# A fused Fourier filter, feed-forward block and expert layer: three steps of the token loop put in another order, and a single-buffered DMA turn in the last pair

## The chip, the core and the metric

The kernel runs on one core of one Trainium2 chip. The metric is the device time of one execution in microseconds. TensorE is called PE here, VectorE DVE, ScalarE ACT, GpSimd POOL and SyncE SP.

## What is computed

```python
def reference(x, filt_r, filt_i, w_in, w_out, g_ln, expert_emb, tau, w1, w2):
    X = np.fft.rfft(x, axis=1)                      # x is 8 x 3072 x 256
    x = np.fft.irfft(X * (filt_r + 1j * filt_i), n=3072, axis=1).reshape(24576, 256)
    h = x @ w_in                                    # 256 -> 1024
    e = np.exp(h - h.max(-1))
    solu = h * e / e.sum(-1)
    ln = (solu - solu.mean(-1)) / np.sqrt(solu.var(-1) + 1e-6) * g_ln
    x = ln @ w_out                                  # 1024 -> 256
    logits = unit(x) @ unit(expert_emb).T / tau     # 8 experts
    k = argmax(logits);  gate = softmax(logits)[k]
    return gate * (relu(x @ w1[k]) @ w2[k])         # 256 -> 1024 -> 256
```

The products are made to nearly float32 accuracy from float16 halves: a value is split into a high half and the remainder, and three products of halves take the place of one.

## The kernel before

The eight sequences are worked on as four pairs. A pair goes through a transform in four stages (64 x 48 points): `fft` holds stages 1 to 3 with the filter between the second and the third, `inv4` is stage 4. Then come 48 tiles of 128 tokens in the token loop `stage_b`, and when all 192 tiles are through, `stage_c` runs the experts, block by block of 256 tokens of one expert.

The token loop (L959) runs over `i`, with two tiles in hand: tile `i`, and tile `j = i - 3`, which is three behind. For a tile:

- `begin` is the first layer: 12 matmuls into `h`, a PSUM tile of which there are two. `top` takes its maximum (DVE, `nm`, L925 and L926) and from it a scale (POOL, `gcc`, L928 and L929).
- the exponential into `es` (ACT, L967), and the product of it with `h` (DVE, also `es`, L968); the sum of its squares (ACT, `jk`, L995).
- `es` has to be turned and split into halves `T` for the second layer. `turn` (L931) does it on PE: 8 transposes back into `h` (L936), the high half on ACT (L939), the low half on DVE (L940). `send` (L942) makes the halves `hl` first, on ACT (L946) and DVE (L947), and `post` (L950) turns both by one DMA transpose from SP (L955). Before, even tiles are turned on PE and odd ones sent by DMA, but all 48 tiles of the last pair are turned on PE.
- the second layer: 24 matmuls into `o` (L983), whose last 8 columns are the logits. Then the square of the row (ACT, L1001), its inverse root as a scale `c2` (POOL, `gcc`, L1009), the logits' copy `graw` (DVE, L1007), and one tile later, in `half`, the row split and stored (`rows`, L1013 and L1014; `put`, L1018).

Stage 4 makes two tiles of tokens at a time, on even `i`: 8 matmuls into a PSUM tile `a` (L740), of which there are two that the transform's stages use as well, then the high half `xh` on ACT (L745) and the low one, `xh` too in the rows, on DVE (L746).

Eight tiles make a group. `b_final` picks their experts and places: a generator that goes a step further with each `i`, some of it on POOL (a reciprocal root in 16 small operations, L808 to L811) and with a small matmul that counts (L851, L853; it reads `goh`). A group marked `slow` takes its POOL work in smaller pieces. Each token's place is scattered into a list in DRAM (L166). One group is marked `snap`: the counts behind it fix the first 24 blocks of the experts, whose table `first_slots` (the generator `early`) reads from the list (L1098, tile `crow`) and whose first block it gathers (L1169) and turns (L1174, tile `cxT`), a step with each `i` from `i >= n - N2 + SPLIT + LAG`, which is 185, on.

Between these, `aux` does other work in two pieces per tile, one ahead of the first layer and one behind it. In the first three pairs that is the next pair's stages 1 to 3 and the maxima of the expert weights (L423); in the last pair it is the split of the expert weights into halves (`w_split`: loads L440 and L442, ACT L462, DVE L454), until tile 38 of the pair. Its loads are two steps ahead.

Nothing reorders this: each engine runs its instructions in the order in which the code issues them, and waits where an input isn't there. What is written ahead of what in the loop is the order on every engine and queue, SP's and POOL's too. Tiles come from pools by tag with a fixed number of buffers. The last pair has its own pool `bp`, in the room that the transforms leave.

```python
            if 0 <= i - 1 < n and i != n - 1:
                (turn if i % 2 or i > n - N2 else send)(i - 1)
```

Of the kernel before, what the change touches and what calls it, by code (L numbers as in the profile page):

```python
# [12 lines left out]
I32 = mybir.dt.int32  # L13
# [140 lines left out]
class Build:  # L154
# [734 lines left out]
    def stage_b(self, xp, bps, gp, ps, hp, op, aux, early):  # L889
# [8 lines left out]
        def over(f, x):  # L898

            while x in (2, 3):  # L900
                x = next(f)
            return x
# [56 lines left out]
        for i in range(n + LAG):  # L959
            j = i - LAG  # L960
            now = 0 <= i < n
            if 0 <= i - 1 < n and i != n - 1:
                (turn if i % 2 or i > n - N2 else send)(i - 1)
            if now:
                L = live[i]
                L["s"] = L["pool"].tile([128, FF], F32, name="es", tag="es")
                nc.scalar.activation(L["s"], L["h"], AF.Exp, bias=L["nm"], scale=self.isc_h[:, i // N2:i // N2 + 1], accum_out=col(i, "st", 0))  # L967
                nc.vector.scalar_tensor_tensor(L["s"], L["h"], col(i, "cc", 0), L["s"], op0=ALU.mult, op1=ALU.mult, accum_out=col(i, "st", 1))  # L968
            if i == n - 1:
                turn(i - 1)  # L970
            if i % 2 == 0:
                xs.append(next(src, None))
            if half:
                half()
                half = None
            self.catch_up()
            if 0 <= j < n:
                T = live.pop(j)["T"]
                o = op.tile([128, 512], F32, name="o", tag="o")
                q = 0  # L980
                for f in range(8):
                    for l, r in ((f, self.wo_h), (f, self.wo_l), (8 + f, self.wo_h)):
                        nc.tensor.matmul(o[:, :D + E], T[:, l, :], r[:, f, :], start=q == 0, stop=q == 23)  # L983
                        q += 1
                self.spot = o[:, 272:344]
                finals = [(f, next(f) if x == 2 else x) for f, x in finals]
            if now:
                if 0 < i <= n - N2 and i % 2 == 0:
                    post(i - 1)
                aux(*divmod(i, N2), 0)  # L990
                if i + 1 < n:
                    begin(i + 1)
                    top(i + 1)
                jk = L["pool"].tile([128, FF], BF16, name="jk", tag="jk")
                nc.scalar.activation(jk, L["s"], AF.Square, accum_out=col(i, "st", 2))  # L995
            if 0 <= j < n:
                n2, c2 = col(j, "n2", 0), col(j, "cc", 1)
                g, k = groups[j // G], j % G
                if k % 2 == 0:
                    rows = gp.tile([128, 2, RD], I32, name="rows", tag="rows", bufs=2)  # L1000
                nc.scalar.activation(rows[:, k % 2, :].bitcast(BF16)[:, :D], o[:, :D], AF.Square, accum_out=n2)  # L1001
# [4 lines left out]
            if 0 <= j < n:  # L1006
                nc.vector.tensor_copy(g["raw"][:, k, :], o[:, D:D + E])  # L1007
                finals = [(f, next(f) if x == 3 else x) for f, x in finals]
                nc.gpsimd.tensor_scalar(c2.bitcast(I32), n2.bitcast(I32), -0.5, float(MAGIC + (8 << 23)), op0=ALU.mult, op1=ALU.add)  # L1009
# [13 lines left out]
                if k == G - 1:  # L1023
                    p, nn = divmod(j - (G - 1), N2)
                    finals.append((self.b_final(groups.pop(j // G), p, nn, gp, ps, j // G == n // G - 4, j // G < n // G - 4), 0))
            if i >= n - N2 + SPLIT + LAG:
# [3 lines left out]
        finals = [(f, over(f, x)) for f, x in finals]  # L1030
# [21 lines left out]
    def table(self, sp, tp, ps, nb, start, K, blk, out):  # L1052
# [48 lines left out]
        assert len(self.scattered["lst"]) >= (self.np_run * N2 // G - (3 if start is None else 0)) * G  # L1101
# [182 lines left out]
    def run(self):  # L1284
        tc, nc = self.tc, self.nc
        last = self.np_run - 1
        with (
# [17 lines left out]
            with (  # L1305
# [3 lines left out]
                with tc.tile_pool(name="pp", bufs=1) as pp:  # L1309
# [7 lines left out]
                    self.m1 += [ap.tile([128, 4, 128], F32, name="mt", tag="mt", bufs=3) for _ in range(2)]  # L1317
# [15 lines left out]
                def last_pool():  # L1333
# [3 lines left out]
                    bps[1] = mid.enter_context(Tags(tc, "bp", {"nm": 2, "es": 2, "jk": 1, "T": 4}))  # L1337
# [84 lines left out]
```

## Time and profile before

| | |
|---|---|
| runs | 2745.77 us median of 3 (2744.71 to 2745.79) |
| the profiled execution | 2744.74 us, span 2742.9 us |
| granted PE clock | 0.986 of full speed |
| busy in the span | PE 2620.9, DVE 1891.5, ACT 1527.3, POOL 1328.7 us |

The span runs from the first instruction to the last; the execution's own time has 1.8 us around it. In the span, the first pair's transform takes the first 200 us, the token loop the time to about 1677 us (its first three pairs, with the transforms beside them, to about 1300, the last pair from there), and the experts the rest.

A row of a timeline gives the start in us, the duration, the engine, the line, the operation, out<-in and the count; in brackets the idle time of the engine just before it and what ended it. The line numbers are those of the kernel before, except in listings of the changed one.

### The profile page before, as it was taken

The numbers are of one execution on the slowest core, as the hardware profiler recorded it, in microseconds if no ns is written. First come the engines' busy times: TensorE is split into PE (matmuls) and PEld (weight loads), VectorE is DVE, ScalarE is ACT, GpSimd is POOL, SyncE is SP. The second block draws the span as 40 slices with busy tenths as digits, with TensorE's granted clock in tenths as the row PEclk, the third lists the DMA queues.
The fourth block names the chain that finished last, engine by engine and source line by source line (L and its number), as shares of the span: only waits on it lengthen the run. The fifth ranks groups of instructions, "written<-read, shape, count | busy, mean of one in ns | idle before, by whom it ended". The sixth has DMA issues, their size and how long they took to land.

```text
span 2742.9 us, 53684 instructions
## 1 busy us (share of the span) xinstructions
PE 2620.9 (96%) x20090; PEld 2024.3 (74%) x20090; DVE 1891.5 (69%) x2971; ACT 1527.3 (56%) x2852; POOL 1328.7 (48%) x2627
## 2 busy tenths in 40 slices
PE   5889999999999999999999998999999999999998
PEld 4447666676666776666776777888888888888897
DVE  4846899868989769888788975454545454454565
ACT  2556788767877767777688863223333333333332
POOL 2000346545566446665555556644444544454444
PEclk7999999999999999999999999999999999999999
DMA  9768888799997989885344422332323332322222
GB/s 313 202 193 244 222 199 199 195 246 209 195 194 161 234 222 198 191 169 138 94 122 122 126 51 56 74 76 73 79 74 78 76 76 77 77 77 76 78 60 57
DMA packets 444118, 384.13 MB, mean 140 GB/s; under 512 B 284779, under 2 KB 366837, under 8 KB 440784
## 3 DMA queue, kind: packets, MB, share of 16 engines
q1 hardware_dynamic: 391200, 310.34, 48.0%
q0 software_dynamic: 26896, 57.21, 6.8%
q10 hardware_dynamic: 25760, 13.14, 1.9%
q8 instruction: 159, 2.61, 0.4%
q14 instruction: 103, 0.84, 0.1%
HBM read 195.67 MB, written 103.09 MB: 109 GB/s over the span
## 4 chain that ended last, share of the span: by engine, by line
PE 39%; issue 23%; POOL 20%; DVE 12%; DMA 4%; ACT 1%; POOLq 0%; SPq 0%; ACTq 0%; DVEq 0%
PE h L758 15%; PE o L983 11%; POOL crow L1169 7%; POOL out_dram L166 6%; POOL scr L165 3%; DVE nm L925 3%; PE a L514 2%; PE a L688 2%; PE h L936 2%; PE a L740 2%; POOL gcc L928 2%; DMA bufA<-out 1%; DVE T L940 1%; DVE in L586 1%; PE a L650 1%
## 5 line engine op out<-in xcount | busy, mean ns | idle before, releaser
L983 PE MATMUL o<-wo_h,T 128*128 128x264 f16 x3072 | 549.6, 276 | 0.1
L928 POOL TENSOR_SCALAR gcc<-nm 128x1 f32<-128x1 f32 x192 | 180.3, 939 | 725.3 <-DVE nm L926 485.7
L758 PE MATMUL h<-win_h,xh 128*128 128x512 f16 x1536 | 492.4, 382 | 35.1 <-DVE T L940 33.5
L1212 PE MATMUL o<-cw,chh 128*128 128x256 f16 x3152 | 522.7, 273 | 0.8 <-issue 0.8
L1245 PEld LDWEIGHTS <-cw 128*128 128x128 f16 x5184 | 471.0, 98 | 58.1 <-issue 8.3
L983 PEld LDWEIGHTS <-T 128*128 128x128 f16 x4608 | 451.0, 98 | 64.4 <-ACT rows L1001 0.3
L758 PEld LDWEIGHTS <-xh 128*128 128x128 f16 x2304 | 222.0, 98 | 317.1 <-issue 84.8
L166 POOL DMA_INDIRECT out_dram<-cot,ids x197 | 215.2, 1092 | 452.9 <-ACT cot L1215 440.6
L1212 PE MATMUL o<-cw,chl 128*128 128x256 f16 x1576 | 429.7, 273 | 3.8 <-DVE chl L1249 3.6
L983 PE MATMUL o<-wo_l,T 128*128 128x264 f16 x1536 | 423.9, 276 | 0.0
L1249 DVE SCALAR_TENSOR_TENSOR chl<-h,chh 128x512 f16<-128x512 f32 x197 | 134.6, 683 | 389.9 <-ACT chh L1248 373.3
L925 DVE TENSOR_REDUCE nm<-h 128x1 f32<-128x1024 f32 x192 | 234.5, 1221 | 150.8 <-PE h L758 150.4
L1212 PEld LDWEIGHTS <-chh 128*128 128x128 f16 x3152 | 307.4, 98 | 36.7 <-issue 1.4
L1215 ACT ACTIVATE cot<-o,fac 128x256 f32<-128x256 f32 x197 | 93.5, 475 | 413.3 <-PE o L1212 407.6
L1201 DVE COPY cw<-wexp 128x4096 f16 x216 | 275.2, 1281 | 41.1 <-PE o L1212 20.7
L1245 PE MATMUL h<-cxT,cw 128*128 128x256 f16 (+1 forms) x2592 | 292.1, 264 | 7.2 <-DMA cxT<-crow 7.1
L758 PE MATMUL h<-win_l,xh 128*128 128x512 f16 x768 | 293.1, 382 | 0.0
L1245 PE MATMUL a<-cxT,cw 128*128 128x256 f16 (+1 forms) x2592 | 291.7, 263 | 0.4 <-issue 0.4
L968 DVE SCALAR_TENSOR_TENSOR es<-h,gcc,es 128x1024 f32<-128x1024 f32 x192 | 245.7, 1280 | 37.0 <-POOL gcc L929 31.9
L967 ACT ACTIVATE es<-h,nm,isc_h 128x1024 f32<-128x1024 f32 x192 | 230.2, 1199 | 31.3 <-DVE nm L926 19.4
L995 ACT ACTIVATE jk<-es 128x1024 bf16<-128x1024 f32 x192 | 202.1, 1052 | 64.2 <-DVE es L968 63.0
L166 POOL DMA_INDIRECT lst<-gdi,gix x192 | 218.1, 1136 | 35.3 <-issue 33.0
(261 smaller groups left out, 4368.7 us busy)
## 6 DMA issues: line engine op xcount, KB each, us to landing
wst<-in_w_dram SPq DMA_DIRECT2D x128, 256.0 KB
in<-in_x_dram SPq DMA_DIRECT2D x48, 512.0 KB
in<-bufA SPq DMA_DIRECT2D x64, 384.0 KB
c<-bufC SPq DMA_DIRECT2D x96, 256.0 KB
xs<-rows SPq DMA_DIRECT2D x96, 256.0 KB
ft<-in_filt_dram SPq DMA_DIRECT2D x24, 960.0 KB
bufA<-out SPq DMA_DIRECT2D x72, 256.0 KB
zw<-z SPq DMA_DIRECT2D x96, 192.0 KB
```

Source lines behind the costliest of these rows:

```text
L166: ins = self.nc.gpsimd.indirect_dma_start(in_offset=None, **kw).ins
L758: nc.tensor.matmul(h[:, nb, :], l[:, i, db, :], r[:, db, sl], start=k == 0, stop=k == 5)
L925: nc.vector.tensor_reduce(x[:, 0:1], L["h"], axis=AX.X, op=ALU.max, negate=True)
L928: nc.gpsimd.tensor_scalar(cc, nm, nm, 1.0, op0=ALU.mult, op1=ALU.max)
L967: nc.scalar.activation(L["s"], L["h"], AF.Exp, bias=L["nm"], scale=self.isc_h[:, i // N2:i // N2 + 1], accum_out=col(i, "st", 0))
L968: nc.vector.scalar_tensor_tensor(L["s"], L["h"], col(i, "cc", 0), L["s"], op0=ALU.mult, op1=ALU.mult, accum_out=col(i, "st", 1))
L983: nc.tensor.matmul(o[:, :D + E], T[:, l, :], r[:, f, :], start=q == 0, stop=q == 23)
L995: nc.scalar.activation(jk, L["s"], AF.Square, accum_out=col(i, "st", 2))
L1169: nc.gpsimd.indirect_dma_start(out=rows[:, h, :], out_offset=None, in_=self.xs, in_offset=bass.IndirectOffsetOnAxis(ap=tab["ids"][:, h, k: ...
L1201: nc.vector.tensor_copy(w.rearrange("p (o k) -> p o k", o=1), self.wexp[:, bass.ds(e, 1), part * 4096:(part + 1) * 4096])
L1212: nc.tensor.matmul(o[:, :D], l[f // fs][:, f % fs, h * 128:(h + 1) * 128], w2[:, r, f, :], start=q == 0, stop=q == 23)
L1245: nc.tensor.matmul(t[:, i, :], w1[:, l, db, f * 128:(f + 1) * 128], xT[:, r + db, :n], start=q == 0, stop=q == 5)
```

## The change

It has four parts. In the token loop, `turn` or `send` of tile `i` moves from the beginning of the next iteration to a place directly behind `begin` and `top` of tile `i + 1`, ahead of the second piece of `aux`. Stage 4 (`next(src)`) moves ahead of the product (L968) and, of tile `j`, the square and the scale `c2` move directly behind the second layer. In the last pair odd tiles are sent by DMA as elsewhere, but for the very last tile; its pool gets one buffer `hl`. And the marked group is one earlier, with the table started three tiles earlier (at 182); at the end of the loop and behind it, a group that has its choice ready no longer issues its counting matmul in the same step. Two buffers that hold constants of the first transform are taken from the tag `wst` where they came from `mt`, of the same size.

```diff
         def over(f, x):
-            while x in (2, 3):
-                x = next(f)
-            return x
+            return next(f) if x == 3 else x
...
         for i in range(n + LAG):
             j = i - LAG
             now = 0 <= i < n
-            if 0 <= i - 1 < n and i != n - 1:
-                (turn if i % 2 or i > n - N2 else send)(i - 1)
             if now:
                 L = live[i]
                 L["s"] = L["pool"].tile([128, FF], F32, name="es", tag="es")
                 nc.scalar.activation(L["s"], L["h"], AF.Exp, bias=L["nm"], scale=self.isc_h[:, i // N2:i // N2 + 1], accum_out=col(i, "st", 0))
-                nc.vector.scalar_tensor_tensor(L["s"], L["h"], col(i, "cc", 0), L["s"], op0=ALU.mult, op1=ALU.mult, accum_out=col(i, "st", 1))
-            if i == n - 1:
-                turn(i - 1)
             if i % 2 == 0:
                 xs.append(next(src, None))
+            if now:
+                nc.vector.scalar_tensor_tensor(L["s"], L["h"], col(i, "cc", 0), L["s"], op0=ALU.mult, op1=ALU.mult, accum_out=col(i, "st", 1))
...
                 finals = [(f, next(f) if x == 2 else x) for f, x in finals]
+                n2, c2 = col(j, "n2", 0), col(j, "cc", 1)
+                g, k = groups[j // G], j % G
+                if k % 2 == 0:
+                    rows = gp.tile([128, 2, RD], I32, name="rows", tag="rows", bufs=2)
+                nc.scalar.activation(rows[:, k % 2, :].bitcast(BF16)[:, :D], o[:, :D], AF.Square, accum_out=n2)
+                nc.gpsimd.tensor_scalar(c2.bitcast(I32), n2.bitcast(I32), -0.5, float(MAGIC + (8 << 23)), op0=ALU.mult, op1=ALU.add)
             if now:
-                if 0 < i <= n - N2 and i % 2 == 0:
+                if i and i % 2 == 0:
                     post(i - 1)
...
                 nc.scalar.activation(jk, L["s"], AF.Square, accum_out=col(i, "st", 2))
-            if 0 <= j < n:
-                n2, c2 = col(j, "n2", 0), col(j, "cc", 1)
...
+                (turn if i % 2 == 0 or i == n - 1 else send)(i)
             if now:
                 aux(*divmod(i, N2), 1)
...
-                    finals.append((self.b_final(groups.pop(j // G), p, nn, gp, ps, j // G == n // G - 4, j // G < n // G - 4), 0))
-            if i >= n - N2 + SPLIT + LAG:
+                    finals.append((self.b_final(groups.pop(j // G), p, nn, gp, ps, j // G == n // G - 5, j // G < n // G - 5), 0))
+            if i >= n - N2 + SPLIT:
                 next(early, 0)
             finals = [(f, x) for f, x in ((f, next(f, 1)) for f, _ in finals) if x != 1]
         self.spot = None
-        finals = [(f, over(f, x)) for f, x in finals]
...
-                    self.m1 += [ap.tile([128, 4, 128], F32, name="mt", tag="mt", bufs=3) for _ in range(2)]
+                    self.m1 += [ap.tile([128, 4, 128], F32, name="wst", tag="wst", bufs=3) for _ in range(2)]
...
-                    bps[1] = mid.enter_context(Tags(tc, "bp", {"nm": 2, "es": 2, "jk": 1, "T": 4}))
+                    bps[1] = mid.enter_context(Tags(tc, "bp", {"nm": 2, "es": 2, "jk": 1, "hl": 1, "T": 4}))
```

How the order moves, at three places. PE near the start of the token loop, behind a first layer, before (the rows of L514 are stage 1 of the next pair, those of L936 the turn):

```order
L758 MATMUL h<-win_h,xh 128x512
L514 MATMUL a<-in,mt 128x256 x2
L936 MATMUL h<-cst,es 128x128 x8
L514 MATMUL a<-in,mt 128x256 x2
L758 LDWEIGHTS xh
```

and in the changed kernel:

```order
L758 MATMUL h<-win_h,xh 128x512
L934 MATMUL h<-cst,es 128x128 x8
L514 MATMUL a<-in,mt 128x256 x4
L758 LDWEIGHTS xh
```

The turn stands directly behind the first layer, and the transform's piece follows it. In all, the turn has 97 such rows where it had 120, and SP 95 DMA transposes of `hl` where it had 72.

DVE in the last pair, from one maximum to the next, before (`wexp` is the split of the expert weights, `T` and `hl` the low halves of a turned and of a sent tile, `xh` stage 4's):

```order
L925 TENSOR_REDUCE nm<-h 128x1
L926 TENSOR_SCALAR nm<-nm,isc_h 128x1
L454 SCALAR_TENSOR_TENSOR wexp<-wst_16103,sc_w,wexp 128x512
L1007 COPY graw<-o 128x8
L940 TENSOR_TENSOR T<-h,T 128x1024
L968 SCALAR_TENSOR_TENSOR es,gst<-h,gcc,es 128x1024
L746 SCALAR_TENSOR_TENSOR xh<-a,ysc,xh 128x512
L1014 SCALAR_TENSOR_TENSOR rows<-o,gcc,rows 128x256
L454 SCALAR_TENSOR_TENSOR wexp<-wst_16128,sc_w,wexp 128x512
```

and now:

```order
L923 TENSOR_REDUCE nm<-h 128x1
L924 TENSOR_SCALAR nm<-nm,isc_h 128x1
L945 TENSOR_TENSOR hl<-es,hl 128x1024
L454 SCALAR_TENSOR_TENSOR wexp<-wst_16069,sc_w,wexp 128x512
L1003 COPY graw<-o 128x8
L746 SCALAR_TENSOR_TENSOR xh<-a,ysc,xh 128x512
L967 SCALAR_TENSOR_TENSOR es,gst<-h,gcc,es 128x1024
L1009 SCALAR_TENSOR_TENSOR rows<-o,gcc,rows 128x256
L454 SCALAR_TENSOR_TENSOR wexp<-wst_16104,sc_w,wexp 128x512
```

The low half has moved ahead of a weight split and a copy, and stage 4's low half ahead of the product; this tile's low half is now that of a sent tile.

POOL at the gather of the experts' first block, before (L1009 is the scale `c2` of a tile, L165 and L166 a scatter into the list, L879 to L883 the end of a group's places):

```order
L1009 TENSOR_SCALAR gcc<-gn_18632 128x1
L1169 DMA crow<-xs,ids_19324 128x256 x2
L165 MEMSET scr 1x1
L166 DMA lst<-gdi,gix 196864x2
L879 IOTA gdi 128x8
L880 TENSOR_TENSOR gdi<-gr,grg 128x8
```

and now (L987 is the scale `c2`, L926 and L927 that of the maximum, L825 and L827 a group's choice at an earlier step):

```order
L987 TENSOR_SCALAR gcc<-gn_18542 128x1
L926 TENSOR_SCALAR gcc<-nm 128x1
L927 TENSOR_SCALAR gcc<-gcc,ccm 128x1
L1163 DMA crow<-xs,ids_19002 128x256 x2
L165 MEMSET scr 1x1
L166 DMA lst<-gdi,gix 196864x2
L825 TENSOR_TENSOR grn<-grn,gr 128x8
L827 TENSOR_TENSOR gd<-graw,grn 128x64
```

The gather stands three tiles earlier, while first layers are still being made, and a tile's `c2` stands ahead of the next tile's maximum.

## Rows read from the trace of the kernel before

**Rows 1.** The page's engine line: busy us, share of the span, instructions.

```profile
PE 2620.9 (96%) x20090; PEld 2024.3 (74%) x20090; DVE 1891.5 (69%) x2971; ACT 1527.3 (56%) x2852; POOL 1328.7 (48%) x2627
```

**Rows 2.** Windows: stretch and length, busy us by engine, PE clock, DMA share, GB/s.

```profile
200.00:1300.00 1100.00, 1065.96 (x6886) 732.12 (x6886) 924.01 (x1508) 832.61 (x1575) 574.73 (x1309) 1.00 0.86 201
650.00:900.00 250.00, 239.32 (x1531) 159.25 (x1530) 228.56 (x360) 195.03 (x369) 156.03 (x313) 1.00 0.89 191
1300.00:1650.00 350.00, 339.52 (x2492) 247.69 (x2490) 294.65 (x568) 264.17 (x506) 189.54 (x556) 1.00 0.41 102
```

**Rows 3.** PE's waits, 200 to 1810 us: total us, times, longest.

```profile
PE h L758 <- DVE T L940: 33.5, 33, 2.9
PE h L1245 <- DMA cxT<-crow: 7.1, 1, 7.1
PE a L650 <- DVE xh L746: 4.4, 4, 2.1
PE a L514 <- DVE xh L746: 3.6, 3, 1.6
PE a L688 <- DVE xh L746: 3.1, 3, 1.2
...
PE h L936 <- DVE es L968: 2.3, 2, 1.4
PE a L851 <- DVE goh L843: 2.1, 1, 2.1
```

**Rows 4.** Timeline of PE in the last pair.

```profile
1453.12 1.04 PE L936 MATMUL h<-cst,es 128*128 128x128 f32 x8
1453.99 0.28 PE L983 MATMUL o<-wo_h,T 128*128 128x264 f16 x1
...
1459.37 1.04 PE L936 MATMUL h<-cst,es 128*128 128x128 f32 x8
```

**Rows 5.** Tile `hl`: durations in ns (min/median/max), first and last start, forms.

```profile
L947 DVE TENSOR_TENSOR hl<-es,hl x72: 1208/1215/1259, 205.3 to 1338.4; 128x1024 f16<-128x1024 f32 x72
```

**Rows 6.** SP's timeline; then the DMA share, 1322 to 1342, 40 slices.

```profile
1326.32 1.77 SPq L955 DMA_TRANSPOSE T<-hl  x1
...
DMA  0069894932099999200000000000098969100299
```

**Rows 7.** Timeline, 674 to 684 us: DVE and PE.

```profile
678.35 1.27 DVE L606 SCALAR_TENSOR_TENSOR zw<-zw,cst,ft 96x1024 f32<-96x1024 f32 x1
...
681.02 1.21 DVE L940 TENSOR_TENSOR T<-h,T 128x1024 f16<-128x1024 f32 x1
...
682.28 0.38 PE L758 MATMUL h<-win_h,xh 128*128 128x512 f16 x1 [2.80 <-DVE T L940]
```

**Rows 8.** Timeline, 462 to 470.5 us: ACT, DVE and PE.

```profile
466.00 0.68 ACT L745 ACTIVATE xh<-a,ysc 128x512 f16<-128x512 f32 x1
...
467.59 1.28 DVE L968 SCALAR_TENSOR_TENSOR es<-h,gcc,es 128x1024 f32<-128x1024 f32 x1 [0.49 <-POOL gcc L929]
...
468.80 0.74 DVE L746 SCALAR_TENSOR_TENSOR xh<-a,ysc,xh 128x512 f16<-128x512 f32 x1
...
469.60 0.47 PE L650 MATMUL a<-hi,d2h 96*96 96x512 f32 x1 [2.06 <-DVE xh L746]
```

**Rows 9.** Timeline, an even tile at 1314 us: ACT, DVE and PE.

```profile
1313.85 0.68 ACT L745 ACTIVATE xh<-a,ysc 128x512 f16<-128x512 f32 x1
...
1314.34 1.28 DVE L968 SCALAR_TENSOR_TENSOR es<-h,gcc,es 128x1024 f32<-128x1024 f32 x1 [0.58 <-POOL gcc L929]
...
1317.06 1.04 PE L936 MATMUL h<-cst,es 128*128 128x128 f32 x8
```

**Rows 10.** Timeline, 1676 to 1684 us, where the experts begin.

```profile
1676.31 0.28 PE L983 MATMUL o<-wo_h,T 128*128 128x264 f16 x1
...
1677.38 0.19 POOL L1009 TENSOR_SCALAR gcc<-gn 128x1 int32<-128x1 int32 x1
...
1679.75 1.23 DVE L1201 COPY cw<-wexp 128x4096 f16 x1 [1.08 <-DMA xs<-rows]
```

More of the change, by code (lines that the diff above doesn't have):

```diff
@@ L995, in stage_b @@
                 nc.scalar.activation(jk, L["s"], AF.Square, accum_out=col(i, "st", 2))
-            if 0 <= j < n:
-                n2, c2 = col(j, "n2", 0), col(j, "cc", 1)
[L998 to L1001, printed above, removed]
+                (turn if i % 2 == 0 or i == n - 1 else send)(i)
             if now:
@@ L1008, in stage_b @@
                 finals = [(f, next(f) if x == 3 else x) for f, x in finals]
-                nc.gpsimd.tensor_scalar(c2.bitcast(I32), n2.bitcast(I32), -0.5, float(MAGIC + (8 << 23)), op0=ALU.mult, op1=ALU.add)
                 def half(j=j, k=k, o=o, c2=c2, rows=rows):
@@ L1100, in table @@
             in_offset=bass.IndirectOffsetOnAxis(ap=ri[:K].bitcast(U32), axis=0)).ins
-        assert len(self.scattered["lst"]) >= (self.np_run * N2 // G - (3 if start is None else 0)) * G
+        assert len(self.scattered["lst"]) >= (self.np_run * N2 // G - (4 if start is None else 0)) * G
         for name in self.scattered["lst"]:
```

## Prediction

> **What bounds the kernel now.** I read four views, from coarse to fine. The page's engine line comes first [rows 1]: PE is busy 2620.9 of 2742.9 us, DVE 69%, so PE sets the pace and 122 us of its idle time is all that waits can give back; anything more has to be PE work taken away. Second, the windows by stage [rows 2]: with the transforms interleaved (200 to 1300 us) PE is busy 1065.96 of 1100 us, in the last pair (1300 to 1650) 339.52 of 350. So 34.0 and 10.5 us are idle there. DVE has 924.01 and 294.65 in the same stretches, 84% in both, but 228.56 of 250 (91%) in the dense stretch from 650 to 900. Third, PE's own list of waits, which runs on into the last stage [rows 3]: 33.5 us for the low half of a turned tile (`T`, DVE) before the next first layer, and 4.4 + 3.6 + 3.1 = 11.1 us for the low half of stage 4 (`xh`, DVE). Together 44.6: that is all of the idle time of the two stages. Fourth, timelines of single waits, to see whether DVE was short of time or only did things in an unlucky order.
>
> **Odd tiles of the last pair turned by DMA.** A turn costs PE the time from its start to the next product's first matmul: 1453.12 to 1453.99, 0.87 us [rows 4]. The order listings count 97 turns where there were 120, and 95 transposes on SP where there were 72. So 23 x 0.87 = 20.0 us of PE work goes. DVE still makes the low half, from SBUF now, at 1215 ns [rows 5] where it took 1.21 us from PSUM [rows 7]; ACT still makes the high one. What is left must fit: PE 339.5 - 20.0 = 319.5 us against DVE's 294.65, so DVE would be 92% busy and PE still the longer. On the DMA side a transpose issued at 1326.32 fills the engines from 1327.5 to 1330 and they are quiet from 1330.5 [rows 6] (slices of 0.5 us): 2.5 us of engine time, landed 4.2 us after issue. 23 x 2.5 = 58 us on top of a DMA share of 0.41 in 350 us makes 0.57. A tile takes 6.25 us here (turn to turn, 1453.12 to 1459.37 [rows 4]); the tile's product comes some 1.5 tiles after the issue, 9.4 us, and the single new `hl` buffer is rewritten two tiles later, 12.5 us. Both leave 5 us and more, so I cost the DMA at nothing. Queued behind the transpose on SP are the weight loads of the splits; SP holds it 1.77 us, they are asked for two half-tile steps ahead (about 6 us), and if that cover fails ACT stands still at the next split, and PE after it.
>
> The Trainium skill ("VectorE: DVE Perf Modes", sections on the three transpose paths and the rules for kernel authors) speaks against this part: it puts a 128x128 bf16 block at 390 ns on TensorE and 1309 ns by DMA, and advises TensorE where PSUM will do as the destination. By it, as an estimate, 16 blocks in a row are 20.9 us, 11.5 us too late per odd tile, and the sum would be some 265 us worse. The trace disagrees: the 16 blocks of a tile are through 4.2 us after the issue [rows 6].
>
> **Splits directly behind the next first layer.** The wait at 682.28 shows what it does [rows 7]. DVE was done with the max of the next tile and free for the low half at 678.35. It began that at 681.02, because it first did a filter product (1.27) and other transform and routing work; PE stood 2.80 us. In the new order the low half ends near 679.6, and PE wanted it at 682.28 - 2.80 = 679.48: the wait shrinks to 0.1. The work it overtakes runs right behind it, and what is late next is that.
>
> **Stage 4's halves ahead of the product.** At 469.60 PE had stood 2.06 us [rows 8]: `xh` was ready at 466.68, but DVE took the product `es` first (467.59 to 468.87) and the low half only after it. Ahead of the product it starts in the 0.49 us that DVE idled there, runs from 467.1 to 467.85, and the wait falls to 0.3; the product, which waited for POOL's `gcc` until 467.59, moves back by 0.3.
>
> For both reorderings the ends are 0 and 44.6 us. In the two examples over 80% goes. In the dense stretch, without its idle 10.7 us, DVE would have 228.56 of 239.3 us to do, 95.5%, so part comes back as other waits for DVE. I take 60%: 26.8 us.
>
> **What the new order can cost.** On the 96 even tiles the product now stands behind the low half of stage 4, and the transposes come directly behind the next first layer. Where nothing else runs [rows 9] `xh` ended at 1314.53 and the product at 1315.62, the turn began at 1317.06. Now: low half 1314.55 to 1315.3, product to 1316.6, still 0.5 us ahead of the turn, cost nothing; with the cover gone it is at most the low half's 0.75 per even tile, 72 us. I take 3 us, by the nearest row, the two waits on `es` that the list does have, 2.3 us [rows 3]; they fall where POOL ran a group's square roots in one piece, and one more group now does.
>
> **The start of the experts.** The first matmul of the last stage waits 7.1 us for `cxT` [rows 3]. The tables start three tiles earlier, some 18 us, so `cxT` is there; next is the weight copy `cw`, which started at 1679.75 [rows 10], after the last tiles' `rows` and `graw`, which stood behind POOL's `gcc` at 1677.38, held up in its turn by gathers and list scatters. That `gcc` now comes before the gathers and right behind its square. The last product matmul starts at 1676.31; 0.3 for it, some 0.8 for the square and the copy of its logits and the 1.08 that DVE idled before `cw` now bring `cw` to 1678.5, its end to 1679.7 and the first matmul to about 1680.0. It ran 7.1 behind the last product and would then run 3.4 behind it: 3.7 us saved (between 0, if `cw` has another wait, and 7.1). A matmul on `goh` that waited 2.1 us in that stage [rows 3] is issued a step later: 2.1. Together 5.8. The two constants' buffers of another tag are of equal size, and no wait of PE in these rows names `mt` or `wst`: nothing.
>
> **Sum.** 20.0 + 26.8 + 5.8 - 3 = 49.6 us. The profiled execution took 2744.74, 1.0 below the median of 2745.77; the same difference from the median gives 2696.
>
> **Rivals.**
> - *DVE becomes the limit.* At 92 to 95% with waits in order, half of the 20.0 and three quarters of the 44.6 return: 10 + 11.1 + 5.8 - 3 = 24 saved, 2722. For it: the dense stretch [rows 2]. Against: PE's remaining work in the last pair is 25 us longer than DVE's.
> - *All waits go*: 20 + 44.6 + 5.8 = 70 saved, 2675. Against it speaks the 95.5%.
> - *The product is late for the turn* (slower). Place: even tiles, DVE between stage 4's low half and the product. It decides once the product ends more than 0.5 us later than worked out, as the transposes then stand at the head of PE's queue with no transform work ahead of them. At the full 0.75 us on 96 tiles: 72 us, 2768. Against: where transforms are interleaved the product waited for POOL anyway [rows 8].
> - *The DMA turn comes late* (slower). If weight loads and transposes queue so that landing takes 12 us where 4.2 was seen, PE stands about 2.4 us (over the 9.4) on each of 23 tiles: 55 us, 2751. Against: a DMA share of 0.57. The rule of the Trainium skill above is this case at its worst, and the landing of 4.2 us speaks against it.
> - That the change does not do what it says is out: the listings show the turns gone and the rows moved.
>
> **Chances and range.** Forecast 0.70 (its own range 2684 to 2710, the reorderings giving 12 to 38 us), DVE limit 0.15, all waits 0.08, late product 0.04, late DMA 0.02, rest 0.01. The range 2680 to 2724 takes in the forecast and the near half of the DVE case and leaves some 0.18 outside. A measurement tells about 0.2%, 5.5 us, from no change; the first three cases lie beyond it on the fast side but for a thin edge, so faster 0.92, same 0.03, slower 0.05.
>
> **What would show it.** Right: 97 turns at 0.87 us; PE's list of waits from 200 to 1650 with `T` and `xh` at some 18 us in all where it was 44.6; the last pair 20 to 25 us shorter; the first matmul of the experts 3.5 us behind the last product; no new wait on the transposes. Wrong: DVE at 95% over the last pair with new PE waits on `T`, `nm` or `es` of 10 us and more there; PE's turn waiting on `es` on most even tiles; ACT or PE waiting on a DMA in the last pair; the experts' start still waiting on `cxT` or on a DMA ahead of `cw`.

## The result, and the profile after

The changed kernel takes 2710.45 us (median of 4 runs, 2709.07 to 2711.76) where the one before took 2745.78 in the same set: a ratio of 0.9866, 95% interval 0.9849 to 0.9883. It is 35.3 us faster; 49.6 was forecast, and the range held. The profiled execution took 2711.44 us with a span of 2709.7.

The page's engine line [rows 1] and three windows [rows 2] of the changed kernel (in a window's row: stretch, its length, then busy time and instructions of PE, PEld, DVE, ACT and POOL, the granted clock, DMA share and GB/s):

```profile
PE 2600.8 (96%) x19906; PEld 1998.1 (74%) x19906; DVE 1886.6 (70%) x2971; ACT 1526.9 (56%) x2852; POOL 1316.1 (49%) x2627
...
200.00:1300.00 1100.00, 1087.90 (x7068) 743.58 (x7068) 940.77 (x1551) 849.62 (x1613) 562.34 (x1348) 1.00 0.89 203
650.00:900.00 250.00, 246.95 (x1585) 163.13 (x1584) 233.71 (x370) 199.30 (x381) 148.64 (x329) 1.00 0.90 195
1300.00:1650.00 350.00, 327.38 (x2383) 234.47 (x2382) 296.69 (x575) 265.42 (x509) 211.39 (x584) 1.00 0.65 134
```

PE has 20.1 us less to do. From 200 to 1300 us it stands 12.1 us, where it stood 34.0. From 1300 to 1650 it stands 22.6, where it stood 10.5; that window now takes in the start of the experts as well.

Fixed times cut the program at different places in the two kernels, so from here on the stretches go from event to event: from the maximum (`nm`) of the first tile to that of tile 143, on to that of tile 191 (the last pair), on to the first matmul of the experts, and to the end. Before:

```profile
191.91:1329.99 1138.08, 1102.23 (x7140) 757.86 (x7140) 953.92 (x1563) 860.08 (x1627) 592.88 (x1361) 1.00 0.85 198
1329.99:1662.09 332.10, 320.26 (x2344) 233.09 (x2342) 278.06 (x530) 249.49 (x477) 180.44 (x537) 1.00 0.39 99
1662.09:1683.67 21.58, 14.42 (x132) 12.31 (x131) 12.45 (x34) 8.34 (x21) 13.23 (x33) 0.93 0.28 62
1683.67:2742.90 1059.23, 1040.28 (x9937) 932.53 (x9937) 538.38 (x683) 329.00 (x592) 526.19 (x657) 0.99 0.29 74
```

and after:

```profile
191.46:1304.51 1113.05, 1098.84 (x7140) 750.79 (x7140) 949.50 (x1564) 857.85 (x1626) 567.16 (x1362) 1.00 0.88 203
1304.51:1625.05 320.54, 303.27 (x2170) 214.83 (x2169) 278.20 (x536) 250.70 (x478) 192.65 (x533) 0.99 0.68 139
1625.05:1643.68 18.63, 13.29 (x122) 11.05 (x120) 10.50 (x27) 9.06 (x22) 12.05 (x32) 1.00 0.29 69
1643.68:2709.70 1066.02, 1040.72 (x9937) 931.98 (x9937) 539.78 (x685) 328.83 (x592) 528.93 (x662) 0.99 0.29 73
```

So 25.0 us came in the first three pairs, 11.6 in the last, 3.0 at the start of the experts, 0.4 ahead of the first tile, and the last stage gave 6.8 back: 33.2 of span. In the last pair PE's busy time fell by 17.0 us and its idle time rose from 11.8 to 17.3; another 3.4 us of busy time went in the first three pairs, where no turn was taken away.

PE's waits, 200 to 1810 us, after (they answer to [rows 3]; total, times, longest):

```profile
PE h L934 <- DVE es L967: 9.6, 11, 1.9
PE o L851 <- DVE goh L843: 8.3, 4, 4.1
PE h L1239 <- DMA cxT<-crow: 5.5, 1, 5.5
...
PE h L1239 <- issue: 3.1, 1, 3.1
PE o L978 <- DVE rows L1009: 2.7, 3, 2.1
PE a L650 <- DVE xh L746: 2.5, 3, 0.9
PE a L688 <- DVE xh L746: 2.1, 2, 1.5
...
PE h L758 <- DVE T L938: 1.5, 2, 0.9
```

`T` went from 33.5 to 1.5. In its place stand `es` (the product, for the turn of an even tile), `goh` (the group's choice, for its counting matmul) and `rows`. No wait names a turned tile's DMA. ACT, however, has a wait that it did not have before; its list over the last pair:

```profile
ACT wexp L462 <- DMA wst<-in_w_dram: 7.9, 4, 3.5
```

**The longest of these waits, link by link.** SP's queue, then ACT, DVE and PE, and the clock around it:

```profile
1513.07 4.85 SPq L953 DMA_TRANSPOSE T<-hl  x1
1518.02 2.56 SPq L442 DMA_DIRECT2D wst<-in_w_dram  x3
```

```profile
1524.68 0.72 ACT L462 ACTIVATE wexp<-wst,sc_w 128x512 f16<-128x512 f32 x1 [3.52 <-DMA wst<-in_w_dram]
...
1526.35 1.04 ACT L944 ACTIVATE hl<-es 128x1024 f16<-128x1024 f32 x1
```

```profile
1527.42 1.23 DVE L945 TENSOR_TENSOR hl<-es,hl 128x1024 f16<-128x1024 f32 x1 [3.42 <-ACT hl L944]
...
1529.80 0.23 DVE L843 TENSOR_TENSOR goh<-gd,go 128x64 f16<-128x64 f32 x1
```

```profile
1530.09 0.24 PE L851 MATMUL o<-goh,c 128*128 128x72 f16 x1 [4.13 <-DVE goh L843]
```

```profile
1515.00:1520.00 5.00, 4.36 (x36) 3.46 (x35) 4.96 (x8) 4.20 (x7) 3.68 (x11) 1.00 1.14 267
1520.00:1525.00 5.00, 5.00 (x36) 3.60 (x35) 3.96 (x9) 1.16 (x4) 3.04 (x10) 1.00 0.83 121
1525.00:1530.00 5.00, 0.96 (x9) 0.59 (x6) 2.51 (x7) 5.00 (x10) 2.07 (x3) 0.97 0.74 202
1530.00:1535.00 5.00, 4.91 (x28) 2.59 (x29) 3.55 (x8) 2.50 (x6) 0.19 (x1) 0.69 0.89 192
```

The transpose sits at the head of SP's queue for 4.85 us with three weight loads behind it. They are issued late, ACT stands 3.52 us at the split, the high half of `hl` is late by that, DVE stands 3.42, the small operations of the group behind it are late, and PE stands 4.13 us. Then the granted clock is 0.69 for a slice of 5 us. The DMA engines are busy as well while this goes on (DMA share 1.14, 0.83 and 0.74 from 1515 on). How much of the loads' lateness is the held queue and how much the busy engines, no run separates.

**A second kind of wait, with no DMA in it.** POOL, ACT, DVE and PE around 1505:

```profile
1502.30 0.22 POOL L809 TENSOR_TENSOR gt<-gt,gt 128x16 f32<-128x16 f32 x1
...
1507.07 0.22 POOL L811 TENSOR_TENSOR gy<-gy,gt 128x16 f32<-128x16 f32 x1
1507.26 0.19 POOL L987 TENSOR_SCALAR gcc<-gn 128x1 int32<-128x1 int32 x1
```

```profile
1507.49 0.47 ACT L1008 ACTIVATE rows<-o,gcc 128x256 f16<-128x256 f32 x1 [2.98 <-POOL gcc L987]
```

```profile
1508.15 1.28 DVE L967 SCALAR_TENSOR_TENSOR es<-h,gcc,es 128x1024 f32<-128x1024 f32 x1 [3.35 <-POOL scr L165]
```

```profile
1509.89 0.27 PE L978 MATMUL o<-wo_h,T 128*128 128x264 f16 x1 [2.06 <-DVE rows L1009]
```

A group that is not marked slow makes its inverse roots in one piece of 16 operations, some 5.3 us, and the scales `gcc` of a tile stand behind them on POOL. (DVE's wait is put down to POOL's `scr`; the operand is `gcc`, made at 1507.86.)

### The profile page after: what moved, and what is told of

It is laid out like the page before. It is cut to its first block, busy times and chain, and to the rows that moved or that the text cites. A ratio compares the mean times of both kernels' runs of the same rounds, so it can differ in the third digit from the quotient of the medians.

```text
span 2709.7 us, 53510 instructions
## 1 busy us (share of the span) xinstructions
PE 2600.8 (96%) x19906; PEld 1998.1 (74%) x19906; DVE 1886.6 (70%) x2971; ACT 1526.9 (56%) x2852; POOL 1316.1 (49%) x2627
## 4 chain that ended last, share of the span: by engine, by line
PE 42%; issue 21%; POOL 17%; DVE 10%; DMA 5%; ACT 5%; POOLq 0%; SPq 0%; DVEq 0%; ACTq 0%; another core or an unknown queue 0%
PE h L758 13%; PE o L978 12%; POOL crow L1163 6%; POOL out_dram L166 6%; POOL scr L165 3%; PE a L688 3%; PE a L514 3%; PE h L934 2%; PE o L1206 2%; PE a L740 2%; DVE es L967 2%; DVE nm L923 2%; DMA bufA<-out 1%; PE a L650 1%; PE h L1239 1%
## 5 line engine op out<-in xcount | busy, mean ns | idle before, releaser
L166 POOL DMA_INDIRECT out_dram<-cot,ids x197 | 210.8, 1070 | 448.1 <-ACT cot L1209 435.5
L926 POOL TENSOR_SCALAR gcc<-nm 128x1 f32<-128x1 f32 x192 | 139.6, 727 | 577.9 <-DVE nm L924 577.7
L1163 POOL DMA_INDIRECT crow<-xs,ids x197 | 199.1, 1011 | 66.2 <-issue 66.2
```

Of the source, the lines that this page charges most:

```text
L166: ins = self.nc.gpsimd.indirect_dma_start(in_offset=None, **kw).ins
L926: nc.gpsimd.tensor_scalar(cc, nm, nm, 1.0, op0=ALU.mult, op1=ALU.max)
L1163: nc.gpsimd.indirect_dma_start(out=rows[:, h, :], out_offset=None, in_=self.xs, in_offset=bass.IndirectOffsetOnAxis(ap=tab["ids"][:, h, k: ...
```

## Experiments

Three theories of why the last pair kept only 11.6 us: **A**, weight loads held up behind the transposes on SP; **B**, the groups' ends, of which one more is now in large pieces; **C**, DVE is simply the limit. The first four runs undo one part of the change each; the others test A, B and C. Sets ran on different chips, and before itself had medians from 2737 to 2746 us, so whole times are compared by ratio or within a set, and mechanisms by the stretches of the profiled execution. Each stretch comes from one profile. The two profiles of the change differ by 3.1 us in the first three pairs, 3.4 in the last pair and 9.7 in the last stage, so a difference of that size does not count by itself; the waits have to bear it out.

| run | median us | before, same set | ratio (95%) | first three pairs | last pair | to the experts | last stage |
|---|---|---|---|---|---|---|---|
| change | 2710.45 | 2745.78 | 0.9866 (0.9849-0.9883) | 1113.1 | 320.5 | 18.6 | 1066.0 |
| change again | 2694.74 | 2737.24 | 0.9843 (0.9826-0.9859) | 1116.2 | 317.1 | 18.6 | 1056.3 |
| 1 turns on PE | 2703.97 | 2745.96 | 0.9846 (0.9833-0.9860) | 1113.9 | 324.6 | 18.1 | 1062.3 |
| 2 splits at head | 2716.44 | 2745.96 | 0.9892 (0.9874-0.9910) | 1126.3 | 319.5 | 18.5 | 1063.6 |
| 3 product first | 2703.34 | 2745.96 | 0.9847 (0.9827-0.9868) | 1120.3 | 314.3 | 18.8 | 1061.2 |
| 4 tables late | 2702.01 | 2745.96 | 0.9834 (0.9818-0.9849) | 1116.0 | 316.0 | 23.4 | 1064.8 |
| 5 loads early | 2688.46 | 2737.24 | 0.9826 (0.9809-0.9842) | 1113.0 | 312.6 | 18.6 | 1055.4 |
| 6 light low split | 2682.1 (one run) | 2737.24 | | 1114.6 | 307.6 | 18.6 | 1057.3 |
| 7 groups slow | 2690.97 | 2737.24 | 0.9830 (0.9814-0.9846) | 1112.9 | 308.6 | 19.5 | 1062.6 |
| 8 loads and groups | 2697.51 | 2742.09 | 0.9847 (0.9826-0.9869) | 1112.9 | 306.6 | 19.5 | 1069.3 |
| 9 product first late | 2697.95 | 2742.09 | 0.9840 (0.9818-0.9861) | 1113.1 | 307.3 | 19.5 | 1066.1 |
| 10 both, PE turns | 2710.31 | 2742.09 | 0.9888 (0.9869-0.9908) | 1114.5 | 322.5 | 20.4 | 1066.6 |
| 11 one group | 2697.82 | 2745.09 | 0.9825 (0.9805-0.9844) | 1112.8 | 308.6 | 22.3 | 1063.2 |

**The change again.** 

> The changed kernel once more, on the chip that runs the experiments of this set. If its profile of before's comparison stands, 2710. If only the start of its profiled execution was long (its first maximum came at 191.5 us, that of the four other variants at 183.0 to 188.3), 2702 to 2706, with the same 1113 us from the first maximum to that of tile 143.

The time lies below both figures. The kernel before is faster on this chip too, by 8.5 of the 15.7 us; the ratio is 0.9843, 42.5 us. The last pair took 317.1 where the first profile has 320.5, ACT waited 2.2 us for weight loads where it waited 7.9, and the last stage took 1056.3. The gain of the change is thus 35 to 43 us, depending on the set; the first three pairs came out 3.1 longer than expected.

**1. Odd tiles of the last pair on PE again.**

```diff
-(turn if i % 2 == 0 or i == n - 1 else send)(i)
+(turn if i % 2 == 0 or i >= n - N2 else send)(i)
-if i and i % 2 == 0:
+if 0 < i <= n - N2 and i % 2 == 0:
     post(i - 1)
```

> The changed kernel, but the last pair's odd tiles are turned on PE again. The prediction's term for them was 20.0 us: 2710.4 + 20 = 2730. Theory A (in the last pair the transposes hold up the weight loads on SP's queue, ACT waits 7.9 us for them and PE behind it, and so only some 10 us of the 20 arrived): 2719 to 2723, and ACT's waits for the loads of the split gone. Theory C (DVE is the limit of the last pair, 94% busy from 1340 to 1410 us): the DMA turn moved the limit from PE to DVE, also 2719 to 2723, but DVE then below 90% and no wait of ACT to explain.

The last pair:

```profile
1297.11:1621.68 324.57, 320.18 (x2354) 233.72 (x2353) 280.52 (x537) 252.58 (x479) 168.08 (x535) 1.00 0.41 102
```

The last pair is 4.0 to 7.5 us longer than with the DMA turn. As a whole the ratio cannot be told from the change's; 9 to 20 us more had been expected by all three. PE has 17 us more to do (320.18 against 303.27) and stands only 4.4 us. ACT has no wait for weight loads. So of the 20.0 us some 4 to 8 arrived in the last pair, and none that shows in the whole. DVE is 86% busy (280.52 of 324.57) and 87 to 88% with the DMA turn; that does not yet tell A, B and C apart.

**2. Turn and send at the head of the next iteration.**

```diff
+if 0 <= i - 1 < n and i != n - 1:
+    (turn if i % 2 or i == n else send)(i - 1)
...
-(turn if i % 2 == 0 or i == n - 1 else send)(i)
```

> The changed kernel, but turn and send of a tile stand at the head of the next iteration again. The prediction gave the two reorderings 26.8 us; by the shares of the waits (33.5 of 44.6 us on T) 20 of them are this one: 2710.4 + 20 = 2730, with PE's waits on T back at 25 to 33 us between 200 and 1650 us. The rival, by which the order of stage 4 and the free time on PE carried it: under 8 us, 2718 or less.

The waits on `T` are back:

```profile
PE h L758 <- DVE T L938: 29.2, 28, 3.5
```

The first three pairs take 1126.3, 10 to 13 us more; the last pair loses nothing. By the ratios the whole is 7 to 13 us slower than the change. 20 was forecast for this part and about half of that is what its loss costs; the rival had said under 8. Other waits may shrink while `T` is late; that was not tried.

**3. Stage 4 behind the product again.**

```diff
+if now:
+    nc.vector.scalar_tensor_tensor(L["s"], L["h"], ...)
 if i % 2 == 0:
     xs.append(next(src, None))
-if now:
-    nc.vector.scalar_tensor_tensor(L["s"], L["h"], ...)
```

> The changed kernel, but stage 4 stands behind the product again. By the prediction 6.7 us (60% of 11.1): 2717, with PE's waits on xh back at some 11 us. The rival, by which the product was behind POOL anyway and what is gained on xh is lost on es: 2710 to 2712. It is faster than the change (2706 or less) if the 8 to 10 us of PE's waits on es come from stage 4 standing ahead of the product.

```profile
PE a L650 <- DVE xh L746: 7.3, 4, 2.6
PE a L688 <- DVE xh L746: 4.3, 3, 2.2
...
PE a L514 <- DVE xh L746: 3.0, 2, 1.5
...
PE h L934 <- DVE es L965: 2.7, 4, 1.6
```

Both answers hold, each in its place. In the first three pairs it costs 4 to 7 us, as forecast (6.7). In the last pair it gives 3 to 6 back, hardly more than the two profiles of the change differ by, with the waits on `es` at 2.7 where they were 9.6 and 6.7. As a whole: no difference.

**4. The table and the marked group late again.**

```diff
-b_final(..., j // G == n // G - 5, j // G < n // G - 5)
+b_final(..., j // G == n // G - 4, j // G < n // G - 4)
-if i >= n - N2 + SPLIT:
+if i >= n - N2 + SPLIT + LAG:
```

> The changed kernel, but the marked group is one later and the table starts three tiles later, as before (the choice of over stays). The prediction gave the start of the experts 5.8 us: 2716, with the first matmul 7 us behind the last product. Theory B (the group of square roots that became quick holds up the scale c2 on POOL and with it PE, about 2 to 4 us, and slot 1's gather gives back 5.5 us): the two cancel, 2709 to 2712, with fewer waits of PE on goh and rows before 1650 us.

```profile
PE o L978 <- DVE rows L1009: 6.4, 2, 4.3
PE h L1239 <- DMA cxT<-crow: 6.2, 1, 6.2
```

The first matmul of the experts waits 6.2 us again and that stretch takes 4.8 us more (23.4 against 18.6): the early table does what was said. The waits on `goh` fall, but one on `rows` of 4.3 us stands in their place, where theory B had said fewer on both; the whole cannot be told from the change's.

**5. Weight loads four steps ahead.**

```diff
-load(0)
-load(1)
+for u in range(4):
+    load(u)
...
-if u < 62:
-    load(u + 2)
+if u < 60:
+    load(u + 4)
...
-tc.tile_pool(name="w2", bufs=4, side="right")
+tc.tile_pool(name="w2", bufs=6, side="right")
```

> The changed kernel with the expert weights loaded four steps ahead in place of two (six buffers). Theory A (the loads land late behind the transposes, ACT's waits for them, 2 to 8 us, are passed on to goh and es): ACT's waits for the loads under 1 us, and from the maximum of tile 143 to that of 191 at least 5 us less than in the changed kernel of the same set. Theories B and C (the groups' ends, or DVE): the waits of ACT go too, but the stretch stays within 2 us.

ACT's list no longer names the loads, and the last pair takes 312.6 us, 4.5 less than the change on the same chip, half a us short of what theory A had named. The wait on `goh` at tile 176, where the chain above ended, is 0.51 where it was 2.18. A is a cause, and a part only: PE still waits 1.70 us for `goh` at tile 168, 2.04 for `rows` at tile 173 and 2.03 for `goh` at 184, the places of B. The median of the whole is 6.3 us below the change's of the same set, but the times overlap (2687.88 to 2690.94 against 2689.11 to 2696.88).

**6. A light low split.**

```diff
-nc.vector.scalar_tensor_tensor(x[:, 2048:2560], w, sc, x[:, :512], op0=ALU.mult, op1=ALU.subtract)
+nc.vector.tensor_copy(x[:, 2048:2560], x[:, :512])
```

> The changed kernel, but the low half of each expert weight is only a copy of the high half: 64 instructions of DVE of 743 ns become about 64 of 0.2 us, and 35 us of DVE's 278 us in the last pair are gone (the output is not the reference's). Theory C (DVE is the limit there): the stretch from the maximum of tile 143 to that of 191 falls to what PE has to do, about 306 us from 316 to 320, with PE's waits there under 5 us. Theories A and B: at most 3 us less, the waits on goh, rows and ACT's on the loads stay.

```profile
1296.78:1604.35 307.57, 301.88 (x2170) 215.27 (x2169) 253.49 (x536) 250.08 (x478) 182.99 (x533) 0.99 0.69 145
```

DVE has 24.7 us less to do (10 less than reckoned) and the pair falls by 9.5 to 307.6, close to what C said. But under A and B the waits were to stay, and they fall: PE's on `goh` from 5.9 to 2.9, on `rows` from 2.4 to 1.2, ACT's on the loads from 2.2 to 1.1. With a lighter DVE the late results reach PE less late, so this run alone does not separate the three.

**7. Two more groups in small pieces.**

```diff
-j // G < n // G - 5
+j // G not in (n // G - 5, n // G - 2, n // G - 1)
```

> The changed kernel, but of the last pair's groups only the marked one and the last two have their ends in few large pieces; two more are spread over more steps as in the earlier pairs. Theory B (POOL's square roots in one piece hold up c2, then rows, es and goh): PE's waits on rows and goh from tile 143 on fall by half and the stretch from the maximum of tile 143 to that of 191 by 4 to 6 us. Theories A and C: within 2 us of the changed kernel of the same set.

The last pair takes 308.6, 8.5 less than the change of the same set, with the waits on `rows` at 0.7 (2.4 in the change again) and on `goh` at 1.7 (5.9). The waits on `goh`, the change again and then this run:

```profile
PE o L851 <- DVE goh L843: 5.9, 3, 2.2
```

```profile
PE o L851 <- DVE goh L843: 1.7, 1, 1.7
```

This is B, more than was expected of it. The ends of the groups now run on into the last stage, which is 6.3 us longer on the same chip; that they are the cause is not shown, as the first profile of the change has 1066.0 us there without them.

**8. Both cures.** The edits of 5 and 7 together.

> The changed kernel with both cures together: the expert weights loaded four steps ahead and two more groups' ends spread over more steps. The cures gave 4.5 and 8.5 us alone between the maxima of tiles 143 and 191 (317.1 us in the changed kernel of that set). If A and B are two causes, 317.1 - 13 = 304 us, within 2 of what PE has to do there (302 to 303). If both only relieve the same few waits: 307 to 309. PE's longest wait in the stretch then stays under 2 us and the granted clock does not fall in it. The whole: 10 us and more faster than the changed kernel.

```profile
1297.55:1604.10 306.55, 300.88 (x2170) 214.69 (x2169) 276.93 (x530) 250.15 (x479) 184.84 (x513) 1.00 0.68 145
```

306.6 is nearer to the 307 of "the same few waits" than to 304, but 2.6 us are less than two profiles differ by. The waits of runs 5 and 7 speak for an overlap: the one at tile 176 falls from 2.18 to 0.51 with the loads early, and it is gone in run 7 too, where ACT still waits 3.4 us for loads. So this wait of PE seems to need both causes. PE stands 5.7 us, 1.70 at the longest. DVE does the same work as in the change (276.93 against 278.16 and 278.20) in 11 to 14 us less, so it was not the limit: C falls. The granted clock stays at 1.00. The whole is no faster than the change, where 10 us and more had been expected; the last stage took 1069.3, and no run without the longer ends was made on that chip.

**9. Product first in the last pair alone,** on top of both cures.

```diff
-if i % 2 == 0:
+if i % 2 == 0 and i < n - N2:
     xs.append(next(src, None))
 if now:
     nc.vector.scalar_tensor_tensor(L["s"], ...)
+if i % 2 == 0 and i >= n - N2:
+    xs.append(next(src, None))
```

> The kernel of both cures, with stage 4 behind the product in the last pair alone (ahead of it in the others). With stage 4 behind the product everywhere the last pair took 314.3 us where the change took 317 to 320, and the pairs before it 1120 where the change took 1113 to 1116. If DVE's order in the last pair is a cause of its own: 2 to 4 us less between the maxima of 143 and 191 than with both cures alone. If it only moved the same waits: within 1 us.

307.3 against 306.6: the order on DVE is no cause of its own there. What run 3 gained in the last pair were then the same waits, or the difference between two profiles.

**10. Both cures, odd tiles on PE.** The edits of 1, 5 and 7.

> The kernel of both cures, but the last pair's odd tiles are turned on PE. This weighs the 20.0 us of the prediction where the collisions are cured: if the term was right and only its cover failed, 318 to 322 us between the maxima of 143 and 191, 14 to 18 more than with both cures and the DMA turn. If the DMA turn has a price of its own there (DMA share near 0.8), the difference stays at 4 to 8 us as in the uncured pair of runs.

```profile
1299.44:1621.93 322.49, 319.62 (x2354) 233.94 (x2353) 279.28 (x531) 252.78 (x479) 157.96 (x515) 1.00 0.42 102
```

With both cures the DMA turn is worth 15.9 us in the last pair (322.5 to 306.6), and 12.8 in the medians of the same set. PE has 18.7 us less to do there (319.62 to 300.88) and stands 5.7 us where it stands 2.9, at a DMA share of 0.68. So the size of the term was nearly right; its cover had failed.

This does not yet make the DMA turn the better choice for the whole. The kernel that turns on PE was no better for the cures: its ratio is 0.9846 without them (run 1) and 0.9888 with them, and the intervals do not touch. Against run 1 the cured kernel with the DMA turn (run 8, 0.9847) gains nothing.

**11. Loads early, one group in small pieces.**

```diff
-j // G < n // G - 5
+j // G < n // G - 3 and j // G != n // G - 5
```

> The changed kernel with the weights loaded four steps ahead and the end of only one more group (the one behind the marked group) spread over more steps. If theory B sits in the square roots of the marked group's neighbours at tile 173 (PE's wait on rows of 2.06 us there, with the granted clock at 0.66 behind it), this one group gives most of what two gave: 307 to 309 us from the maximum of tile 143 to that of 191 (306.6 with both, 312.6 with the loads alone), the waits on goh at tiles 168 and 184 (1.70 and 2.03) stay. The last stage, which took 1069 us with both groups' ends drawn out, is then back at 1055 to 1062. If the later group was the one that counted: 311 to 313.

308.6, with 1.70 and 2.04 us at tiles 168 and 184 left and tile 173's gone: the group behind the marked one carries most of B. Of the 4.0 us less than run 5, 2.0 are PE's busy time (303.11 to 301.10), as the granted clock fell behind that wait in run 5. The last stage took 1063.2, 1.2 over the upper end expected, and PE waited 3.48 us for `es` at the last tile, so the way to the experts is 3.7 longer. Runs 5 and 11 have the best ratios (0.9826, 0.9825). Both beat before for certain; against the change only run 5 has a set in common, with 6.3 us, and the ratio intervals overlap. They overlap with that of run 1 (0.9833 to 0.9860) as well: that the DMA turn gains anything in the whole is not shown, in the last pair it is.

## Why the prediction was right, and where it was off

The sign, the range and the mechanisms of the gain held; 14.3 us of the forecast gain were missing in the first set, 7.1 in the second. The first profile and run 1 divide its 33.2 us: the two reorderings 32.5 (26.8 forecast), the turns less the new costs 4.0 (17.0), the start of the experts 3.0 (5.8, of which 2.1 lay in the last stage), 0.4 ahead of the first tile, and the last stage took back 6.8 (not in the sum). That the errors did not all go one way is luck. Of the signs, 97 turns, the waits on `T` and `xh` (6.7 us, some 18 forecast) and the first matmul of the experts came as said. The last pair is 11.6 to 15.0 us shorter where 20 to 25 was said, and one sign of being wrong came true: ACT waits for a DMA in the last pair.

- **Turns, 20.0.** The count of turns was right. PE's 20.1 us less are near the term by chance: 17.0 of them lie in the last pair, and with the cures, at the full clock, it is 18.7. Of this 4 to 8 us reached the time of the last pair (run 1), 15.9 with the cures (run 10). The step that failed is "so I cost the DMA at nothing", and in it "SP holds it 1.77 us". That came from one transpose in a calm place [rows 6]. The line of all transposes stood in the trace of before (shortest, median and longest in ns), and in the change it is longer still:

```profile
L955 SPq DMA_TRANSPOSE T<-hl x72: 1337/2438/6388, 206.5 to 1339.6; - x72
```

```profile
L953 SPq DMA_TRANSPOSE T<-hl x95: 1317/3188/7100, 205.8 to 1622.4; - x95
```

  The 24 of the last pair, in the change:

```profile
L953 SPq DMA_TRANSPOSE T<-hl x24: 1317/3031/4854, 1313.8 to 1622.4; - x24
```

  None of these is longer than the some 6 us of lead that the loads have. The longest, 4.85, was enough all the same, as the loads behind it have to land too: issued from 1518.02 on, they let ACT go on at 1524.68. Their time on the DMA engines was sized too low as well: a DMA share of 0.57 was forecast from 1300 to 1650 and 0.65 measured. That is some 3.7 us for each of the 23 transposes (0.65 less 0.41, of 350 us) where 2.5 had been read. The sentence on what is late next (ACT at the split, PE after it) was borne out; it needed a price. The landing of the transpose itself was in time, as said. The Trainium skill ("VectorE: DVE Perf Modes", rules for kernel authors) prefers TensorE for a 128x128 transpose where PSUM will do as the destination. The runs do not bear this out in the last pair, where the DMA turn is 4 to 16 us shorter; in the whole they leave it open (runs 10 and 11).
- **The two reorderings, 26.8.** 25.0 us in the first three pairs of the first profile and 21.9 in the second. In the last pair run 1, which has PE's turns as before, takes 324.6 where before took 332.1: another 7.5 us. Together 29 to 33, above the forecast. The 40% that was held back for a busy DVE did not come: from 650 to 900 us DVE is 93% busy (233.71 of 250) and PE 99%. Alone, the splits' place is worth 10 to 13 us (run 2) and stage 4's 4 to 7 (run 3); what is left of the 22 to 25 lies in undoing both together or in the square and scale `c2`, which were not undone.
- **New costs, 3.** Between the cured and the uncured last pair lie 11 to 14 us (306.6 against 317.1 and 320.5). They are the shortfall of the turns seen from the other side, and not a second loss. The step that failed is "the nearest row, the two waits on `es` that the list does have, 2.3 us", with "one more group now does" behind it. Those two waits were taken while PE had 20 us more to do in the pair. With that work gone PE reaches the same late results earlier and stands there. Run 1 shows it: in the same order, with the added quick group but with PE's turns, PE waits 2.2 us on `es`, 1.1 on a group's choice and none on `rows`, where the change has 6.0, 7.9 and 2.5 in the last pair.
- **The start of the experts, 5.8.** The first matmul came 3.1 us behind the last product (3.4 was said), 0.1 behind the end of `cw`, which was named as next. The stretch is 3.0 us shorter, and run 4 gives 4.8 for it. The 2.1 us on `goh` are gone there, but waits on `goh` stand in the last pair.
- **The last stage** was left out of the sum. It gave back 6.8 us in the first set, 5.5 of it one wait for the second block's `cxT`; in the second set that wait was 0.8 and the stage took 1056.3 us. Over all variants it lies between 1055 and 1069. Before's last stage was profiled on one chip only, so how much of this is the change's is open.
- **Rivals.** DVE as the limit (2722): its 10 us in the last pair were lost, but to waits in order, not to DVE's load (run 8). All waits go: 29 to 33 of the 44.6 us went. The product late for the turn: its place was right, its size 9.6 us of waits where 72 was the end. The DMA turn late: no wait of PE on it. Its price was also summed too low: 12 less 9.4 is 2.6 us a tile, 60 us in place of 55.

## What to carry to other kernels

When work leaves the busiest engine, its old waits are no measure of the new ones: it comes sooner to every late result, so list what lands last per step and ask by how much. A transfer that is hidden itself can still hold its queue; price the queue by the longest of all its like and the landing of what stands behind it, not by one calm row, and load that further ahead. Compare each way at its best: the turn on PE did better without the cures. Work in large pieces on a side engine should be cut small where the main engine has lost its slack; look then at where its tail ends (here in the last stage, at a price that was not settled).

## What the runs showed of the chip

Some short waits of PE cost more than their length, because the granted clock was down afterwards. In the change again PE stood 2.18 us, and the next slice had a granted clock of 0.66:

```profile
1520.21 0.21 PE L851 MATMUL o<-goh,c 128*128 128x72 f16 x1 [2.18 <-DVE goh L843]
```

```profile
1520.00:1525.00 5.00, 4.79 (x24) 2.17 (x25) 3.26 (x8) 2.62 (x7) 0.19 (x1) 0.66 0.99 176
```

In the slices where the changed kernel shows it best, 1530 to 1533 us, the granted clock is 0.50, that is 1.2 GHz for the 2.4 GHz of the stretch before, and two matmuls of 128x512 took 1.06 us where they took 0.59. PE's busy time in the last pair is 305.25 us in the change again and 300.88 in run 8, with the same 2170 matmuls. Not every such wait did it: the one of 2.06 us at 1509.89 was followed by a clock of 1.00, and so was one of 2.80 us in the kernel before [rows 7]. Which waits do was not tried.

The sent tiles have a price on POOL that nobody had counted. POOL's scale of the maximum (`gcc`, L926) in the last pair, in the change again and then in run 1, where the odd tiles are turned on PE:

```profile
L926 POOL TENSOR_SCALAR gcc<-nm 128x1 f32<-128x1 f32 x48 | 30.0, 625 | 70.0 <-DVE nm L924 69.9
```

```profile
L926 POOL TENSOR_SCALAR gcc<-nm 128x1 f32<-128x1 f32 x48 | 14.5, 302 | 93.0 <-DVE nm L924 92.9
```

The mean is 625 ns against 302. In the change again those that run beside a turned tile's low half (`T`) took 0.29 to 0.31 us, and those beside a sent tile's (`hl`) 1.18 in the mean and 1.79 at the longest. The prediction compared the two low halves on DVE alone, where they take the same time. How much of this reaches PE, whose even turns wait on the product behind that scale, was not tried.
